# A gated attention and MLP decode step on one core: the first weight load in two transfers, TensorE's loop in eleven rounds, the output weight in other parts

## The chip, the core and the metric

The kernel runs on one core of one Trainium2 chip. The core has five engines with instruction streams of their own: TensorE (PE in the profile, with its weight loads as PEld), VectorE (DVE), ScalarE (ACT), GpSimd (POOL) and SyncE (SP). Data comes from device memory (HBM) by DMA: here every transfer is issued by SyncE, and the work of one transfer is spread over the core's 16 DMA engines. The on-chip memory that the engines read (SBUF) has 128 partitions, which are the rows of every tile.

The metric is the device time of one execution in microseconds. Before the change it is 676.03 us, the median of three runs (675.99 to 676.4).

## The reference

One decode step for two sequences (B = 2), one new token each, with a model width of D = 448. Branch A is attention over a cache of 4096 positions with 16 heads of 256, branch B is an MLP with a ReLU, and a gate mixes the two:

```python
def _A_ref(x, k_cache, v_cache, wq, wo):
    q = (x @ wq).reshape(B, Sq, H, Dh) -> (0, 2, 1, 3)
    scores = einsum("bhqd,bhkd->bhqk", q, k_cache) * Dh ** -0.5
    p = softmax(scores)
    o = einsum("bhqk,bhkd->bhqd", p, v_cache)
    return o @ wo
def _B_ref(x, w1, w2):
    return maximum(x @ w1, 0) @ w2
g = sigmoid((x * gate_w).sum(-1))
out = g * _A_ref(...) + (1 - g) * _B_ref(...)
```

Everything is float32. The caches are by far the largest inputs: 2 x 16 x 4096 x 256 elements each, 134 MB for the keys and as much for the values.

## The kernel before

**Units.** A unit is one head of one sequence; there are U = 32. The host lays the keys and values of a unit side by side as one block of 128 rows with 16,384 floats each (65,536 bytes a row, 8.4 MB a unit). Three buffers of that size, `slot[0]` to `slot[2]` (`slot_49`, `slot_50` and `slot_51` in the instruction listings below), fill most of SBUF.

**The start.** SyncE issues three transfers at once (lines 67 to 69): the query weight `wq` with the input `x` and the gate weight in its last columns, 128 rows of 14,348 floats, into `slot[0]`; then unit 0 into `slot[1]` and unit 1 into `slot[2]`. When `wq` has landed, VectorE copies `x` in a repeated layout to `xr` (L336), TensorE computes the gate (L196) and in two halves the queries (L207), and ScalarE stores them in `qt`. When TensorE is done with `wq`, SyncE loads unit 2 into `slot[0]` (L160).

**The loop.** For each unit, TensorE multiplies the keys by the query (`unit_pe`, L121), VectorE takes the maximum (L135), ScalarE the exponential (L128) and copies the next unit's query (L130), and VectorE multiplies the values by the weights and sums them, in eight instructions (L141). The last of these counts the semaphore `freed` up; on that SyncE issues the transfer of the unit three later into the buffer that came free (L166). The engines' loops run `LOOP = 10` rounds of three units, and the last two units stand written out behind the loop.

**The end.** The last unit's block is loaded as two halves (L171, L172). When unit 29's buffer `slot[0]` is free, the MLP's weights `wm` follow into it in two halves (L174, L175); when unit 30's buffer `slot[1]` is free, the output weight `wo` follows in parts (L179), each with a semaphore of its own in `wo_in`. `wo` has 32 chunks of 448 columns, 1,792 bytes a row. The lists `ACC` and `DIRECT` set the parts: chunks of `ACC` are multiplied into the accumulator `acc` (L276), four chunks at a time in four column groups of TensorE, on top of the MLP's second product (L264); `acc` is copied to `a_sb` (L368) and its four groups are folded into `z` (L284); chunks of `DIRECT` are multiplied straight into `z`, each in four pieces of 112 columns (L289). Then `z` is copied (L370) and 16 of its rows are stored (L182).

**What sets the order.** The program is written out by hand: each engine's stream runs in the order of the code, and semaphores tie the streams together. SyncE's transfers all go to one DMA queue in the order in which they are issued.

The last rows of the width need care: 448 is three times 128 and 64 more. The three full blocks go through a contraction over 128 partitions (`KF = 3`). For the fourth, half a block, the host puts two halves of a weight's columns on top of each other, and `rows_of` picks the upper or the lower 64 partitions.

Of the kernel before, what the change touches and what calls it, by code (L numbers as in the profile page):

```python
# [13 lines left out]
CW = 512  # L14
ACC = (14, 9)
DIRECT = (4, 2, 2, 1)
FOLD_AT = 0


def gated_mix_decode(nc, wq, kv, wm, wo, out):  # L20
# [41 lines left out]
    slot_in = [ev() for _ in range(SLOTS)]  # L62
    last_v, w1_in, w2_in = ev(), ev(), ev()
    wo_in = [ev() for _ in ACC + DIRECT]
    scored, maxed, raised, queried, freed = (ev() for _ in range(5))

    sp.dma_start(slot[0][:, :wq.shape[1]], wq).then_inc(slot_in[0], 16)  # L67
    sp.dma_start(slot[1], kv[0]).then_inc(slot_in[1], 16)
# [5 lines left out]
    fold = sb("fold", P, RB, B)  # L74
    xr = sb("xr", P, KC, P // B, B)
    ge = sb("ge", P, 1)
# [24 lines left out]

    def rows_of(c, i=0):
        return slice(0, P) if c < KF else slice(i * HP, (i + 1) * HP)

    def x_of(r, c, n=R):
        return xr[r, c].rearrange("p r b -> p (r b)")[:, :n]

    xg = slot[0][:, NW:wq.shape[1]].rearrange("p (c b) -> p c b", c=KC)

    ident_0, ident_ok, par_ok = ev(), ev(), ev()  # L110
    x_ok, gate_mm, gate_ok, ge_ok, gp_ok, omg_ok = (ev() for _ in range(6))
# [32 lines left out]

    LOOP = (U - 2) // SLOTS
    U1 = LOOP * SLOTS

# [7 lines left out]
    with nc.Block(no_gpsimd_drain=True) as block:  # L155

        @block.sync
        def _(_e):
            sp.wait_ge(q_mm, 2)
            sp.dma_start(slot[0], kv[2]).then_inc(slot_in[0], 16)  # L160
            with nc.Fori(0, LOOP - 1, engines=(ET.SP,)) as r:
# [12 lines left out]
            sp.dma_start(w1, wm[:, :W1]).then_inc(w1_in, 16)  # L174
            sp.dma_start(w2, wm[:, W1:]).then_inc(w2_in, 16)  # L175
            sp.wait_ge(freed, U - 1)
            k = 0
            for n, s in zip(ACC + DIRECT, wo_in):
                sp.dma_start(w_o[:, k * D:(k + n) * D], wo[:, k * D:(k + n) * D]).then_inc(s, 16)  # L179
                k += n  # L180
            sp.wait_ge(res_ok, 1)
            sp.dma_start(out, res[0:7 * 15 + 1:7, :]).then_inc(out_sem, 16)  # L182

        @block.gpsimd
        def _(_e):
            pool.memset(ident, 0.0).then_inc(ident_0, 1)
            pool.wait_ge(ident_0, 1)
# [3 lines left out]
        @block.tensor  # L191
        def _(_e):
            pe.wait_ge(x_ok, 1)
            for c in range(KC):
                r = rows_of(c)
                m = pe.matmul(pa[:, :1], x_of(r, c, P), xg[r, c, B:], start=(c == 0), stop=(c == KC - 1))  # L196
            m.then_inc(gate_mm, 1)
            W = 2 * KF * DH
            for i in range(2):
                w = slot[0][:, i * NW // 2:(i + 1) * NW // 2]  # L200
                if i:
                    pe.wait_ge(q_ok, i)
                for c in range(KC):
                    for g in range(G):
                        r = rows_of(c, g // 2)
                        at = g * W + c * CW if c < KF else G * W + g % 2 * CW
                        m = pe.matmul(pb[g * R:(g + 1) * R, :], x_of(r, c), w[r, at:at + CW], start=(c == 0),  # L207
                                      stop=(c == KC - 1))
                m.then_inc(q_mm, 1)
                pe.wait_ge(q_ok, i + 1)  # L210
# [6 lines left out]
                m.then_inc(q_tr, 1)  # L217
            with nc.Fori(0, LOOP, 1, engines=(ET.PE,)) as r:
                for k in range(SLOTS):
                    s = (k + 1) % SLOTS  # L220
                    unit_pe(k, r * SLOTS + (k + 1), r * 16 + (32 if s == 0 else 16), s)
            for k in range(U - U1):
                s = (k + 1) % SLOTS
                unit_pe(k, U1 + k + 1, LOOP * 16 + 16, s)

            half = W1 // 2

            def hidden(lo, hi):
                for c in range(lo, hi):
                    for g in range(G):  # L230
                        j, i = divmod(g, 2)
                        at = i * half + (j * KF + c if c < KF else 2 * KF) * FG
                        r = rows_of(c, j)
                        m = pe.matmul(pa[g * R:(g + 1) * R, :FG], x_of(r, c), w1[r, at:at + FG], start=(c == 0),  # L234
                                      stop=(c == KC - 1))
                return m

# [4 lines left out]
            pe.transpose(pc[:U, P:2 * P], ls, ident).then_inc(ml_tr, 1)  # L242
            hidden(2, 3)
# [3 lines left out]
            hidden(3, 4).then_inc(hid_mm, 1)  # L247
            pe.wait_ge(os_ok, 1)
# [31 lines left out]
            for i, a in enumerate(DIRECT):  # L280
                if i == FOLD_AT:
                    pe.wait_ge(a_ok, 1)
# [4 lines left out]
                for _ in range(a):  # L287
                    for g in range(G):
                        m = pe.matmul(z[g * R:(g + 1) * R, :DG], o_of(k),  # L289
                                      w_o[:, k * D + g * DG:k * D + (g + 1) * DG], start=(k == n and FOLD_AT > 0),  # L290
                                      stop=(k == NO - 1))
                    k += 1
            m.then_inc(z_mm, 1)

        @block.scalar
        def _(_e):
# [10 lines left out]
            act.activation(qc[:, 1, :], qt[:, 0, :], AF.Copy).then_inc(queried, 1)  # L307
            with nc.Fori(0, LOOP, engines=(ET.Activation,)) as r:
                u0 = act.snap(r * SLOTS)
# [19 lines left out]
        def _(_e):  # L329
# [5 lines left out]
            dve.wait_ge(slot_in[0], 16)  # L335
            dve.tensor_copy(xr, xg[:, :, None, :B].to_broadcast([P, KC, P // B, B])).then_inc(x_ok, 1)  # L336
            dve.wait_ge(gate_ok, 1)
# [4 lines left out]
            dve.tensor_scalar(omg, gp, -1.0, 1.0, op0=ALU.mult, op1=ALU.add).then_inc(omg_ok, 1)  # L342
            with nc.Fori(0, LOOP, engines=(ET.DVE,)) as r:
                u0 = dve.snap(r * SLOTS)
# [86 lines left out]
```

## Time and profile before

| what | before |
|---|---|
| median of three runs | 676.03 us (675.99 to 676.4) |
| the profiled execution's own time | 675.96 us |
| its span, first to last instruction | 674.4 us |
| TensorE busy | 218.0 us (32%) |
| VectorE busy | 340.4 us (50%) |
| ScalarE busy | 46.3 us (7%) |
| data moved | 289.61 MB, 429 GB/s over the span |
| DMA queue of SyncE, share of 16 engines | 99.3% |

The profiled execution's own time lies 1.56 us above its span; that is time ahead of the first instruction and behind the last that the profile doesn't show. Times in the profile count from the span's start. A row of a group reads: line, engine, operation, result <- operands, shapes and how many; behind the bar the busy time, the mean of one in ns, and the idle time ahead of them with what ended it. In a row of a timeline, the first number is the start and the second the length, in us.

### The profile page before, as it was taken

The numbers are of one execution on the slowest core, as the hardware profiler recorded it, in microseconds if no ns is written. First come the engines' busy times: TensorE is split into PE (matmuls) and PEld (weight loads), VectorE is DVE, ScalarE is ACT, GpSimd is POOL, SyncE is SP. The second block draws the span as 40 slices with busy tenths as digits, with TensorE's granted clock in tenths as the row PEclk, the third lists the DMA queues.
The fourth block names the chain that finished last, engine by engine and source line by source line (L and its number), as shares of the span: only waits on it lengthen the run. The fifth ranks groups of instructions, "written<-read, shape, count | busy, mean of one in ns | idle before, by whom it ended". The sixth has DMA issues, their size and how long they took to land.

```text
span 674.4 us, 3971 instructions
## 1 busy us (share of the span) xinstructions
PE 218.0 (32%) x1309; PEld 53.4 (8%) x1309; DVE 340.4 (50%) x563; ACT 46.3 (7%) x107; POOL 0.7 (0%) x6
## 2 busy tenths in 40 slices
PE   0733221333332123333322233333222333332445
PEld 0200000000000000000000000000000000000012
DVE  0024566545455665544656654455666445456760
ACT  0010000000000000000000000000000000000110
POOL 0000000000000000000000000000000000000000
PEclk9975667767655666766666676665567667655869
DMA  9999999999999999999999999999999999999997
GB/s 381 428 436 435 436 435 435 435 435 435 435 435 435 435 435 435 435 435 435 431 435 435 435 435 435 435 435 435 435 431 435 435 435 435 435 435 408 423 439 303
DMA packets 6084, 289.61 MB, mean 429 GB/s; under 512 B 704, under 2 KB 832, under 8 KB 1216
## 3 DMA queue, kind: packets, MB, share of 16 engines
q1 hardware_dynamic: 6080, 289.55, 99.3%
q8 instruction: 3, 0.05, 0.0%
q14 instruction: 1, 0.01, 0.0%
HBM read 289.54 MB, written 0.01 MB: 429 GB/s over the span
## 4 chain that ended last, share of the span: by engine, by line
DMA 70%; DVE 13%; PE 10%; issue 6%; ACT 1%; DVEq 1%; SPq 0%; ACTq 0%
DMA slot<-in_kv 65%; DVE slot L141 11%; PE sc L121 9%; DMA slot<-in_wo 4%; DVE nm L135 2%; ACT p L128 1%; DVEq L141 1%; PE acc L276 0%; PE z L289 0%; SPq L166 0%; DVE a_sb L368 0%; DVEq L135 0%; ACTq L128 0%; PE z L284 0%; SPq L67 0%
## 5 line engine op out<-in xcount | busy, mean ns | idle before, releaser
L121 PE MATMUL sc<-slot,qc 128*32 128x512 f32 x1024 | 187.2, 898 | 413.1 <-DMA slot<-in_kv 413.1
L141 DVE SCALAR_TENSOR_TENSOR slot<-slot,p 128x1024 f32<-128x1024 f32 x256 | 295.9, 1222 | 47.2 <-ACT p L128 45.8
L135 DVE TENSOR_REDUCE nm<-sc 128x1024 f32 (+1 forms) x32 | 39.2, 1225 | 243.4 <-PE sc L121 243.4
L121 PEld LDWEIGHTS sc<-slot,qc 128*32 128x32 f32 x1024 | 42.0, 156 | 557.6 <-issue 538.6
L128 ACT ACTIVATE p<-sc,nm 128x1024 f32<-128x1024 f32 x32 | 35.6, 1113 | 563.2 <-DVE nm L135 563.2
L141 DVE DVE_READ_ACCUMULATOR slot<-slot,p (+1 forms) x256 | 21.3, 83 | 0.0
L207 PE MATMUL pb<-slot,xr 128*32 128x512 f32 (+1 forms) x64 | 9.5, 732 | 0.0
L336 DVE COPY xr<-slot 128x512 f32<-128x512 f32 x1 | 0.4, 426 | 17.9 <-DMA slot<-in_wq 17.9
L234 PE MATMUL pa<-slot,xr 128*32 128x448 f32 (+1 forms) x32 | 5.2, 761 | 12.3 <-DMA slot<-in_wm 12.3
L196 PE MATMUL pa<-slot,xr 128*128 128x1 f32 (+1 forms) x8 | 2.0, 357 | 20.7 <-DVE xr L336 20.7
L368 DVE COPY a_sb<-acc 128x448 f32<-128x448 f32 x1 | 0.6, 625 | 14.0 <-PE acc L276 14.0
L276 PE MATMUL acc<-slot,oc 128*32 128x448 f32 x46 | 5.6, 542 | 4.2 <-DMA slot<-in_wo 4.2
L128 ACT ACTIVATION_READ_ACCUMULATOR p<-sc,nm (+1 forms) x32 | 6.2, 193 | 0.0
L130 ACT ACTIVATE qc<-qt 128x2 f32 (+1 forms) x31 | 5.9, 192 | 0.0
L264 PE MATMUL acc<-slot,hr 128*32 128x448 f32 x28 | 3.2, 541 | 1.0 <-ACT hr L323 1.0
L196 PEld LDWEIGHTS pa<-slot,xr 128*128 128x128 f32 (+1 forms) x8 | 1.9, 322 | 20.7 <-DVE xr L336 20.7
L207 PEld LDWEIGHTS pb<-slot,xr 128*32 128x32 f32 (+1 forms) x64 | 2.0, 129 | 5.9 <-issue 5.9
L276 PEld LDWEIGHTS acc<-slot,oc 128*32 128x32 f32 x46 | 1.7, 109 | 8.1 <-issue 5.8
L234 PEld LDWEIGHTS pa<-slot,xr 128*32 128x32 f32 (+1 forms) x32 | 0.9, 140 | 14.8 <-DMA slot<-in_wm 13.2
L289 PE MATMUL z<-slot,oc 128*32 128x112 f32 x72 | 1.9, 259 | 0.0
L301 ACT ACTIVATE q<-pb 128x512 f32<-128x512 f32 x2 | 1.2, 597 | 9.1 <-PE pb L207 9.1
L364 DVE COPY oc<-pc 128x256 f32<-128x256 f32 x4 | 1.4, 418 | 0.7 <-PE pc L251 0.7
(45 smaller groups left out, 16.9 us busy)
## 6 DMA issues: line engine op xcount, KB each, us to landing
slot<-in_kv SPq DMA_DIRECT2D x2, 4096.0 KB, 34.9
slot<-in_wq SPq DMA_DIRECT2D x1, 7174.0 KB, 19.4
slot<-in_wm SPq DMA_DIRECT2D x2, 3136.0 KB, 31.2
slot<-in_wo SPq DMA_DIRECT2D x1, 3136.0 KB, 24.6
slot<-in_wo SPq DMA_DIRECT2D x1, 2016.0 KB, 29.0
slot<-in_wo SPq DMA_DIRECT2D x1, 896.0 KB, 30.7
slot<-in_wo SPq DMA_DIRECT2D x2, 448.0 KB, 31.6
slot<-in_kv SPq DMA_DIRECT2D x31, 39.7
```

The costliest lines, as they stand in the source:

```text
L121: m = pe.matmul(sc[g * R:(g + 1) * R, c * CW:(c + 1) * CW], qc[:, s, t:t + 1].to_broadcast([P, R]), slot[s][:, lo:lo + CW], start=(t == 0) ...
L128: act.activation(p, sc, AF.Exp, bias=nm[:, bass.ds(u, 1)], accum_out=ls[:, bass.ds(u, 1)]).then_inc(raised, 1)
L130: act.activation(qc[:, s_next, :], qt[:, bass.ds(u + 1, 1), :].rearrange("p o t -> p (o t)"), AF.Copy).then_inc(queried, 1)
L135: dve.tensor_reduce(nm[:, bass.ds(u, 1)], sc, axis=AX.X, op=ALU.max, negate=True).then_inc(maxed, 1)
L141: m = dve.scalar_tensor_tensor(v, v, 1.0, p, op0=ALU.mult, op1=ALU.mult, accum_out=ov[:, bass.ds(u, 1), j].rearrange("p o -> p o"))
L196: m = pe.matmul(pa[:, :1], x_of(r, c, P), xg[r, c, B:], start=(c == 0), stop=(c == KC - 1))
L207: m = pe.matmul(pb[g * R:(g + 1) * R, :], x_of(r, c), w[r, at:at + CW], start=(c == 0), stop=(c == KC - 1))
L234: m = pe.matmul(pa[g * R:(g + 1) * R, :FG], x_of(r, c), w1[r, at:at + FG], start=(c == 0), stop=(c == KC - 1))
L264: pe.matmul(acc[g * R:(g + 1) * R, :D], hr[:, k, :], w2[:, k * D:(k + 1) * D], start=(k < G), stop=False)
L276: m = pe.matmul(acc[g * R:(g + 1) * R, :D], o_of(k), w_o[:, k * D:(k + 1) * D], start=False, stop=(k >= n - G))
L289: m = pe.matmul(z[g * R:(g + 1) * R, :DG], o_of(k), w_o[:, k * D + g * DG:k * D + (g + 1) * DG], start=(k == n and FOLD_AT > 0), stop=(k = ...
L364: m = dve.tensor_copy(oc[:, h], pc[:, h * B * J:(h + 1) * B * J].rearrange("p (o b j) -> p j o b", o=1, b=B) .to_broadcast([P, J, RB, B]))
```

## The change

There are four edits.

1. **wq in two transfers.** The first 16 rows (`FIRST`) are a transfer of their own with the semaphore `wq_in`; the other 112 rows follow as a second transfer on `slot_in[0]`. VectorE waits for both ahead of its first copy.
2. **The last half block as one contraction.** Instead of four products over 64 partitions, two over 128 partitions, each for 64 rows of the result: the left operand is the new tile `xl`, in which the other half is zero, and the host lays the weight's last columns out for it. A helper, `project`, serves the queries and the MLP's first product. `xr` keeps the three full blocks; VectorE makes `xl` and a small tile `xn` for the gate with three more copies, and GpSimd zeroes `xl`.
3. **TensorE in eleven rounds.** TensorE's loop covers all 32 units; in the last round a branch skips the third unit. The two units that stood written out behind it are gone. The other engines keep ten rounds and two units behind them (`LOOP` is now 11, and they run `LOOP - 1`).
4. **wo in other parts.** 14, 8 and 4 chunks go through `acc` and 3, 2 and 1 straight into `z`, where it was 14 and 9, and 4, 2, 2 and 1. There are six transfers as before.

```diff
-ACC = (14, 9)
-DIRECT = (4, 2, 2, 1)
-FOLD_AT = 0
+FIRST = 16
+ACC = (14, 8, 4)
+DIRECT = (3, 2, 1)
...
-    sp.dma_start(slot[0][:, :wq.shape[1]], wq).then_inc(slot_in[0], 16)
+    sp.dma_start(slot[0][:FIRST, :wq.shape[1]], wq[:FIRST]).then_inc(wq_in, 16)
+    sp.dma_start(slot[0][FIRST:, :wq.shape[1]], wq[FIRST:]).then_inc(slot_in[0], 16)
...
+    def project(dst, w, at, at_last, n, lo, hi):
+        for c in range(lo, min(hi, KF)):
+            for g in range(G):
+                m = pe.matmul(dst[g * R:(g + 1) * R, :n], x_of(c), w[:, at(c, g):at(c, g) + n], start=(c == 0), stop=False)
+        if hi == KC:
+            for i in range(2):
+                m = pe.matmul(dst[i * HP:(i + 1) * HP, :n], xl.rearrange("p j r b -> p (j r b)"),
+                              w[:, at_last(i):at_last(i) + n], start=False, stop=True)
+        return m
...
-    LOOP = (U - 2) // SLOTS
-    U1 = LOOP * SLOTS
+    LOOP = -(-U // SLOTS)
+    FULL = U - (LOOP - 1) * SLOTS
+
+    U1 = (LOOP - 1) * SLOTS
...
-            with nc.Fori(0, LOOP, 1, engines=(ET.PE,)) as r:
-                for k in range(SLOTS):
-                    s = (k + 1) % SLOTS
-                    unit_pe(k, r * SLOTS + (k + 1), r * 16 + (32 if s == 0 else 16), s)
-            for k in range(U - U1):
-                s = (k + 1) % SLOTS
-                unit_pe(k, U1 + k + 1, LOOP * 16 + 16, s)
+            with nc.Fori(0, LOOP, engines=(ET.PE,)) as r:
+                u0 = pe.snap(r * SLOTS)
+
+                def units(lo, hi):
+                    for k in range(lo, hi):
+                        unit_pe(k, u0 + (k + 1), r * 16 + (32 if k == SLOTS - 1 else 16), (k + 1) % SLOTS)
+
+                units(0, FULL)
+                with pe.If_lt(pe.to_reg(r), LOOP - 1):
+                    units(FULL, SLOTS)
+                pe.end_ifs()
...
-            dve.tensor_copy(xr, xg[:, :, None, :B].to_broadcast([P, KC, P // B, B])).then_inc(x_ok, 1)
+            dve.wait_ge(wq_in, 16)
+            dve.tensor_copy(xr, xg[:, :KF, None, :B].to_broadcast([P, KF, P // B, B]))
+            dve.tensor_copy(xn, xg[:, KF:, :B].to_broadcast([P, P // B, B]))
+            dve.wait_ge(xl_0, 1)
+            for j in range(2):
+                m = dve.tensor_copy(xl[j * HP:(j + 1) * HP, j], xg[j * HP:(j + 1) * HP, KF:, :B]
+                                    .to_broadcast([HP, RB, B]))
+            m.then_inc(x_ok, 1)
```

The order of the instructions moves at three places. The first is SyncE's start; `e` with a number is a semaphore, and the 128x14348 block is `wq`. Before:

```order
L67 DMA slot_49<-in_wq 128x14348 [waits barrier_Pool_Activation_PE_DVE_SP_release]
L68 DMA slot_50<-in_kv 128x16384
L69 DMA slot_51<-in_kv 128x16384
L157 UNCONDITIONAL_BRANCH
L160 DMA slot_49<-in_kv 128x16384 [waits e26]
```

And now, on the same engine:

```order
L67 DMA slot_49<-in_wq 16x14348 [waits barrier_Pool_Activation_PE_DVE_SP_release]
L68 DMA slot_49<-in_wq 112x14348
L69 DMA slot_50<-in_kv 128x16384
L70 DMA slot_51<-in_kv 128x16384
L169 UNCONDITIONAL_BRANCH
L172 DMA slot_49<-in_kv 128x16384 [waits e28]
```

One transfer more stands ahead of the two units, and the first of the two touches 16 partitions alone.

The second place is TensorE's loop; the products into `sc` are a unit's 16, and `e0`, `e1` and `e2` count the landings of the three buffers. Before, the loop's third unit, its end and the first of the two units behind it:

```order
L115 REGISTER_ALU
L116 REGISTER_ALU [waits e0]
L121 MATMUL sc<-slot_49,qc 32x512 [waits e15]
L121 MATMUL sc<-slot_49,qc 32x512 x15
L218 REGISTER_ALU
L218 COMPARE_AND_BRANCH
L121 MATMUL sc<-slot_50,qc 32x512 [waits e15,e1]
L121 MATMUL sc<-slot_50,qc 32x512 x15
```

Now, from the loop's second unit to its end and the first instruction behind it:

```order
L131 MATMUL sc<-slot_51,qc 32x512 x15
L233 COMPARE_AND_BRANCH
L125 REGISTER_ALU
L126 REGISTER_ALU [waits e0]
L131 MATMUL sc<-slot_49,qc 32x512 [waits e16]
L131 MATMUL sc<-slot_49,qc 32x512 x15
L233 UNCONDITIONAL_BRANCH
L225 REGISTER_ALU
L225 COMPARE_AND_BRANCH
L111 MATMUL pa<-slot_49,xr 32x448 [waits e5]
```

Two branches stand around the third unit, and the MLP's first product follows the loop directly.

The third place is TensorE's end, from the second part of `wo` on; before, `e7` to `e11` are the landings of `wo`'s second to sixth part, and `e45` is VectorE's copy to `a_sb`:

```order
L276 MATMUL acc<-slot_50,oc 32x448 [waits e7]
L276 MATMUL acc<-slot_50,oc 32x448 x8
L284 MATMUL z<-a_sb,fold 32x112 [waits e45]
L284 MATMUL z<-a_sb,fold 32x112 x3
L289 MATMUL z<-slot_50,oc 32x112 [waits e8]
L289 MATMUL z<-slot_50,oc 32x112 x15
L289 MATMUL z<-slot_50,oc 32x112 [waits e9]
L289 MATMUL z<-slot_50,oc 32x112 x7
L289 MATMUL z<-slot_50,oc 32x112 [waits e10]
L289 MATMUL z<-slot_50,oc 32x112 x7
L289 MATMUL z<-slot_50,oc 32x112 [waits e11]
L289 MATMUL z<-slot_50,oc 32x112 x3
```

Now, with `e8` to `e12` as those landings and `e47` as the copy:

```order
L281 MATMUL acc<-slot_50,oc 32x448 [waits e8]
L281 MATMUL acc<-slot_50,oc 32x448 x7
L281 MATMUL acc<-slot_50,oc 32x448 [waits e9]
L281 MATMUL acc<-slot_50,oc 32x448 x3
L289 MATMUL z<-a_sb,fold 32x112 [waits e47]
L289 MATMUL z<-a_sb,fold 32x112 x3
L294 MATMUL z<-slot_50,oc 32x112 [waits e10]
L294 MATMUL z<-slot_50,oc 32x112 x11
L294 MATMUL z<-slot_50,oc 32x112 [waits e11]
L294 MATMUL z<-slot_50,oc 32x112 x7
L294 MATMUL z<-slot_50,oc 32x112 [waits e12]
L294 MATMUL z<-slot_50,oc 32x112 x3
```

Three chunks have moved from the products into `z` (nine chunks of four pieces) to those into `acc`, ahead of the copy and the fold; the last part is still one chunk.

More of the change, by code (lines that the diff above doesn't have):

```diff
@@ L160, in _ @@
             sp.dma_start(slot[0], kv[2]).then_inc(slot_in[0], 16)
-            with nc.Fori(0, LOOP - 1, engines=(ET.SP,)) as r:
+            with nc.Fori(0, LOOP - 2, engines=(ET.SP,)) as r:
                 u0 = sp.snap(r * SLOTS)
@@ L199, in _ @@
             for i in range(2):
-                w = slot[0][:, i * NW // 2:(i + 1) * NW // 2]
                 if i:
                     pe.wait_ge(q_ok, i)
[L203 to L209, printed above, removed]
+                project(pb, slot[0][:, i * NW // 2:(i + 1) * NW // 2], lambda c, g: g * W + c * CW,
+                        lambda i: G * W + i * CW, CW, 0, KC).then_inc(q_mm, 1)
                 pe.wait_ge(q_ok, i + 1)
@@ L217, in _, with pe_tail @@
                 m.then_inc(q_tr, 1)
[L218 to L224 removed]
+            with nc.Fori(0, LOOP, engines=(ET.PE,)) as r:
[7 more added lines that the diff above has]
+                pe.end_ifs()
+        def pe_tail():
             half = W1 // 2
             def hidden(lo, hi):
[L229 to L236, printed above, removed]
+                return project(pa, w1, lambda c, g: g // 2 * half + (g % 2 * KF + c) * FG,
+                               lambda i: i * half + 2 * KF * FG, FG, lo, hi)
             pe.wait_ge(w1_in, 16)
@@ L289, in _ @@
                         m = pe.matmul(z[g * R:(g + 1) * R, :DG], o_of(k),
-                                      w_o[:, k * D + g * DG:k * D + (g + 1) * DG], start=(k == n and FOLD_AT > 0),
+                                      w_o[:, k * D + g * DG:k * D + (g + 1) * DG], start=False,
                                       stop=(k == NO - 1))
@@ L307, in _ @@
             act.activation(qc[:, 1, :], qt[:, 0, :], AF.Copy).then_inc(queried, 1)
-            with nc.Fori(0, LOOP, engines=(ET.Activation,)) as r:
+            with nc.Fori(0, LOOP - 1, engines=(ET.Activation,)) as r:
                 u0 = act.snap(r * SLOTS)
@@ L342, in _ @@
             dve.tensor_scalar(omg, gp, -1.0, 1.0, op0=ALU.mult, op1=ALU.add).then_inc(omg_ok, 1)
-            with nc.Fori(0, LOOP, engines=(ET.DVE,)) as r:
+            with nc.Fori(0, LOOP - 1, engines=(ET.DVE,)) as r:
                 u0 = dve.snap(r * SLOTS)
@@ L410 @@
     full, last = blocks(B_w1)
-    full = full.reshape(P, KF, 2, 2, FG).transpose(0, 3, 2, 1, 4).reshape(P, 2, -1)
-    last = last.reshape(HP, 2, 2, FG).transpose(1, 0, 2, 3).reshape(P, 2, FG)
+    full = full.reshape(P, KF, 2, 2, FG).transpose(0, 2, 3, 1, 4).reshape(P, 2, -1)
+    last = last.reshape(HP, 2, 2, FG).transpose(2, 0, 1, 3).reshape(P, 2, FG)
     w1 = np.concatenate([full, last], 2).reshape(P, -1)
```

35 lines of the change are left out of this document (20 added, 15 removed).

## The prediction

> **What bounds the kernel now.** I read the page's utilization part first, then the waits, then DMA by stretches, and last the chain of the end.
>
> ```profile
> span 674.4 us, 3971 instructions
> PE 218.0 (32%) x1309; PEld 53.4 (8%) x1309; DVE 340.4 (50%) x563; ACT 46.3 (7%) x107; POOL 0.7 (0%) x6
> ...
> q1 hardware_dynamic: 6080, 289.55, 99.3%
> q8 instruction: 3, 0.05, 0.0%
> ...
> DMA 70%; DVE 13%; PE 10%; issue 6%; ACT 1%; DVEq 1%; SPq 0%; ACTq 0%
> ...
> L121 PE MATMUL sc<-slot,qc 128*32 128x512 f32 x1024 | 187.2, 898 | 413.1 <-DMA slot<-in_kv 413.1
> ```
>
> No engine is busy for more than half of the span, while SyncE's queue holds the 16 DMA engines for 99.3% of it. TensorE stands idle for 413.1 us, all of it waiting for a unit to land. So the kernel lasts as long as its bytes do, plus what lies ahead of the first byte and behind the last.
>
> ```profile
> DMA packets 4320, 251.62 MB, mean 434 GB/s; under 512 B 479, under 2 KB 479, under 8 KB 479
> ...
> q1 hardware_dynamic: 4318, 251.59, 100.1%
> ...
> 660.00:662.00 2.00, 0.00 (x0) 0.00 (x0) 0.00 (x0) 0.00 (x0) 0.00 (x0) 1.00 1.02 436
> 669.00:670.00 1.00, 0.34 (x1) 0.00 (x0) 0.62 (x1) 0.00 (x0) 0.00 (x0) 1.00 0.85 333
> 670.00:671.00 1.00, 0.94 (x40) 0.94 (x44) 0.01 (x1) 0.00 (x0) 0.00 (x0) 1.00 0.23 90
> 671.00:672.00 1.00, 1.00 (x52) 0.94 (x40) 0.00 (x0) 0.00 (x0) 0.00 (x0) 1.00 0.05 18
> ```
>
> The first two lines are the stretch from 20 to 600 us: 251.59 MB in 580 us at a share of 1.001 make 251.59 / (1.001 x 16 x 580) = 27.1 GB/s for one of the 16 engines. The packets say how a transfer is shared out: 251.59 MB are some 3,839 rows of 65,536 B, and 479 packets are small; that is 128 rows and 16 small packets for each of 30 transfers, so every engine carries 8 rows and closes with a small packet. In the last four lines (the last two columns are DMA share and GB/s), the queue runs dry: at 670 to 671 us a share of 0.23 still moves 90 GB/s, or 90 / (0.23 x 16) = 24.5 GB/s for each busy engine, in packets of a few kB. An engine gets no faster when three quarters of them rest. So the limit isn't one that all 16 share. It is either the engine's own or that of the group of partitions it writes. In every large transfer here one engine goes with one share of the 128 partitions, so these rows can't tell the two apart. The forecast hangs on that.
>
> **The first transfer.** Before, `wq` is one transfer:
>
> ```profile
> 0.75 0.39 SPq L67 DMA_DIRECT2D slot<-in_wq  x1
> ...
> slot<-in_wq SPq DMA_DIRECT2D x1, 7174.0 KB, 19.4
> ...
> out<-res SPq DMA_DIRECT2D x1, 7.0 KB, 1.7
> ...
> q1 hardware_dynamic: 32, 0.01, 1.8%
> ```
>
> It lands at 0.75 + 19.4 = 20.15 us; its 7.35 MB take 16.9 us at 434 GB/s, so about 3.2 us pass without bytes. One row is 7174 KB / 128 = 57,392 B, 2.12 us of an engine. The last two rows are the kernel's own transfer of 16 rows, the result: 32 packets, so 16 rows with 16 small packets; sixteen rows, too, go to 16 engines, one each. The new first transfer thus keeps all 16 engines busy, each with one row, but all of them write to partitions 0 to 15.
>
> If the limit is the engine's own, this costs nothing: 2.12 us for the first rows, seven rows on each engine behind them, the same total. SyncE issues one transfer more (0.39 to 0.43 us), which puts unit 0's issue at some 1.65 us in place of 1.2; cover is the first row, which runs past 4 us. A gain at the start is bounded by the 3.2 us without bytes less the 1.14 us at which the first issue is over: 0 to 2.1 us. The nearest row, the store of 16 rows, needs 1.7 us from issue to landing for 7 KB, so a small transfer doesn't begin at once either; I take 0.
>
> If the limit belongs to groups of partitions, sixteen ways of 27.1 GB/s serve 128 partitions, eight each. Sixteen neighbours then lie on anything from 16 ways (dealt out one by one) down to two (eight neighbours on each): the first rows take between 2.12 and 8 x 2.12 = 16.95 us. Until they are done the other ways stand idle, and since each way must still carry its sixteenth of all bytes at a rate that it already holds for 99% of the span, that idle time comes back in full at the end: 0 with 16 ways, up to 16.95 us with two. Of the doublings 16, 8, 4 and 2, I take four ways, in the upper middle: four rows on each, 4 x 2.12 = 8.47 us. The second transfer gives each engine 7 rows, which fit neither groups of 4 nor of 8, so two engines meet on a way now and then. That costs from 0 to 7 x 2.12 = 14.8 us where they meet on all seven; I take one row, 2.1 us, near the low end, because engines that meet fall out of step and then meet less. Together +10.6 us.
>
> The Trainium skill, SBUF — State Buffer, section "Door 1: The DMA port swizzle (why `[64,N]` ≈ `[32,N]`)", says that DMA bandwidth goes by how many of 16 SBUF ports the partitions reach, that four consecutive partitions share one, and that partitions 0 to 15 reach four ports, measured at 104 GB/s. By it the first 0.92 MB would take 8.8 us (an estimate from that page's figure). No run here shows it, and the trace agrees only in that one engine's rate is what the page gives for one port.
>
> I side with the groups. For the engine's own limit speaks only that it is the simpler reading; for the groups speaks that every busy engine in the trace holds one rate to the end, and that all transfers before were spread over all partitions, so that this kernel never ran the other case.
>
> **The projections.** Each half of the queries takes 28 instructions in place of 32 (12 products of two passes and two more, for 16), the MLP's first product the same. VectorE makes four copies for one of 0.43 us, under 1 us more at worst. Cover is the wait for unit 0:
>
> ```profile
> 20.21 0.43 DVE L336 COPY xr<-slot 128x512 f32<-128x512 f32 x1 [17.94 <-DMA slot<-in_wq]
> ...
> 39.64 5.61 PE L121 MATMUL sc<-slot,qc 128*32 128x512 f32 x32 [4.87 <-DMA slot<-in_kv]
> ```
>
> TensorE waits 4.87 us for unit 0, so neither gain nor loss reaches the end: 0. A later `wq` leaves that cover, since unit 0 is behind it in the same queue and comes later by as much. In the MLP's product TensorE waits for `wo` afterwards: 0. GpSimd's zeroing of `xl` has 18 us.
>
> **The loop.** Two branches and a few register instructions in each of ten rounds, well under 1 us a round, fall into the 413.1 us of waiting (12.9 us a unit): 0. TensorE's program loses two units of 32 passes with their weight loads, 128 instructions, and some 60 more at the ends. The page has three fetches of instructions (the q8 row) of 16 KB; one may go. The stretch of the end has two of them:
>
> ```profile
> q8 instruction: 2, 0.03, 0.3%
> ```
>
> That is 630 to 674.4 us, so 0.003 x 16 x 44.4 = 2.1 us for two, about 1.1 us of one DMA engine each. At the end the slowest engines are some 1.4 us behind the rest (share 0.23 and 0.05 above). Removing one of three such delays helps only if it sat on the very last engine, from 0 to 1.4 us; with two fetches left I take 0.
>
> **The end.** The chain behind the last transfers:
>
> ```profile
> 637.84 29.02 DMA slot<-in_wo
> 666.86 0.04 issue
> 666.90 2.46 PE acc L276 x18
> 669.36 0.02 issue
> 669.38 0.64 DVE a_sb L368
> 670.02 0.04 issue
> 670.06 0.40 PE z L284 x8
> 670.46 1.77 PE z L289 x72
> 672.23 0.02 issue
> 672.25 0.28 DVE res L370
> ...
> L179 SPq DMA_DIRECT2D slot<-in_wo x6: 328/432/433, 637.5 to 639.7; - x6
> ...
> slot<-in_wo SPq DMA_DIRECT2D x1, 896.0 KB, 30.7
> slot<-in_wo SPq DMA_DIRECT2D x2, 448.0 KB, 31.6
> slot<-in_wo SPq DMA_DIRECT2D x1, 224.0 KB, 32.0
> ```
>
> Chunk 23 lands at 666.86, chunk 27 at about 638.3 + 30.7 = 669.0, so a chunk takes 0.54 us and chunk 26, the new end of `ACC`, lands at about 668.5. Four chunks are 8 passes at 2.46 / 18 = 0.14 us, done at 669.6 (0.24 us later than now); copy and fold follow (0.64 + 0.40 and two hops), to 670.7; then 48 passes for 72 at 1.77 / 72 = 0.025 us, to 671.9. The last chunk lands at 639.7 + 32.0 = 671.7 as before, since bytes, rows and number of parts are the same, and its 8 passes and the latency of the last one end by 672.1 to 672.2. So the chain of products, which now ends at 672.23, stops being what comes last by 0.05 us, and the landing takes over: -0.05.
>
> **Sum.** The profiled execution took 675.96 us; its median of runs stands 0.07 above it. 675.96 + 10.6 - 0.05 + 0 (projections, loop, fetch) = 686.5 us.
>
> **The rivals.**
>
> *No change.* If 27.1 GB/s is the engine's own limit, 675.96 - 0.05 = 675.9 us, with 0.4 us either way for the start. For it: the busy engines keep their rate, and the bytes and parts are equal.
>
> *Faster.* The rows flow as soon as the first short issue is over, or the fetch that goes was the one on the last engine: up to 2.1 or 1.4 us off, so down to 673.8 us. Against it: both need the whole bound; it is faster by over 0.2% only from 1.35 us on.
>
> *Slower in another way.* If the skipped third unit made TensorE's stream fetch anew in every round, ten fetches of 1.1 us on one DMA engine give +11 us, 687 us; spread over the engines they give about +1. The Trainium skill, Runtime: NRT & Kernel Launch, section "Instruction fetch mechanics", has a taken branch to outside the loaded window force a fetch of the target page. Against it here: ten rounds with a taken branch at each end came with three fetches in all (the q8 row).
>
> **How the numbers follow.** Groups of partitions 0.58; no change 0.34; faster 0.05; fetches 0.03. The likeliest gives 686.5 us; its own range goes from eight ways (4.24 us idle, no meeting) at 680 to two ways at 693. Over all cases, 675.0 to 691.0 leaves out the faster case, a little of no change, and the worst of the groups, some 0.15 in all. 0.2%, or 1.35 us, is about what a measurement of this kernel can tell from no change: faster 0.05, same 0.34, slower 0.61.
>
> **What would show it.** If the groups limit, DMA in the stretch from 4 to 10 us falls to about a quarter of 434 GB/s, `wq` lands at 28 us or later instead of 20.2, VectorE's first copy stands there, units land some 10 us later throughout at the same 434 GB/s, and the end looks as before, shifted. If `wq` lands at 20.2 us again, the groups are wrong and the time is 675.9. More than three q8 packets would show the fetches. For the end, the last products into `z` should follow the last landing by under 0.1 us, and the copy to `a_sb` should come some 0.2 us later against the last landing than now. What would make the forecast wrong is above all that a way into SBUF carries more than one engine brings, or that the first rows don't share one.

## The result and the profile after

The changed kernel takes 694.01 us, the median of four runs (693.39 to 695.05), against 676.1 us before (675.99 to 676.4, also four runs). The ratio is 1.0265, with a 95% interval of 1.0253 to 1.0277: 17.9 us slower. The forecast was 686.5 us: it had the direction and the kind of mechanism, but its range ended at 691.

The profiled execution's span is 692.1 us, 17.7 us longer than before. Its page shows where the time isn't:

```profile
span 692.1 us, 3931 instructions
PE 217.9 (31%) x1279; PEld 52.7 (8%) x1279; DVE 340.9 (49%) x566; ACT 46.4 (7%) x107; POOL 0.8 (0%) x7
...
GB/s 159 265 417 421 432 428 451 443 428 424 424 436 451 443 428 424 424 436 451 443 424 428 424 436 451 443 424 428 424 432 447 451 424 428 424 432 432 431 431 296
...
q1 hardware_dynamic: 6096, 289.55, 99.2%
q8 instruction: 3, 0.05, 0.0%
...
L131 PE MATMUL sc<-slot,qc 128*32 128x512 f32 x1024 | 186.9, 897 | 411.6 <-DMA slot<-in_kv 411.6
```

TensorE has 30 instructions less, the engines are busy as before, the bytes are the same, and TensorE's wait for units even fell by 1.5 us. What differs are the first two of the forty slices: 159 and 265 GB/s, where every later one but the last holds 417 or more. Note the share of the queue: 99.2%, as if nothing were wrong. A packet that takes longer still counts as a busy engine, so the share doesn't show that the engines are slow.

The stretches of the start say it more closely (the last two columns are DMA share and GB/s; bytes count where their packet begins):

```profile
0.00:10.00 10.00, 0.00 (x0) 0.00 (x0) 0.74 (x3) 1.28 (x1) 0.79 (x7) 1.00 1.09 161
10.00:38.00 28.00, 0.00 (x0) 0.00 (x0) 0.00 (x0) 0.00 (x0) 0.00 (x0) 1.00 0.93 242
...
60.00:600.00 540.00, 163.96 (x896) 36.69 (x892) 293.43 (x476) 36.33 (x84) 0.00 (x0) 0.62 1.00 435
```

From 10 to 38 us the queue holds the engines for 0.93 of their time and moves 242 GB/s; from 60 us on it is the old rate. Before the change, the first 20 us were:

```profile
0.00:10.00 10.00, 0.00 (x0) 0.00 (x0) 0.74 (x3) 1.28 (x1) 0.70 (x6) 1.00 0.91 367
10.00:20.00 10.00, 0.00 (x0) 0.00 (x0) 0.00 (x0) 0.00 (x0) 0.00 (x0) 1.00 1.09 472
```

The issues of `wq` and VectorE's first copy (from the timeline and the list of DMA issues; in the latter the last number is us from issue to landing):

```profile
0.75 0.41 SPq L67 DMA_DIRECT2D slot<-in_wq  x1
1.22 0.41 SPq L68 DMA_DIRECT2D slot<-in_wq  x1
...
slot<-in_wq SPq DMA_DIRECT2D x1, 6277.2 KB, 37.7
slot<-in_wq SPq DMA_DIRECT2D x1, 896.8 KB, 11.0
...
38.92 0.55 DVE L347 COPY xr<-slot 128x384 f32<-128x384 f32 x1 [36.64 <-DMA slot<-in_wq]
```

The sixteen rows land at 0.75 + 11.0 = 11.8 us and the other 112 at 1.22 + 37.7 = 38.9 us. Before, all 128 had landed at 20.15 us. So 18.7 us are lost by the time `wq` is there, and 17.7 of them are still there at the end.

### The profile page after: what moved, and what is told of

The parts are those of the page before. It is cut to its first block, busy times and chain, and to the rows that moved or that the text cites. A ratio compares the mean times of both kernels' runs of the same rounds, so it can differ in the third digit from the quotient of the medians.

```text
span 692.1 us, 3931 instructions
## 1 busy us (share of the span) xinstructions
PE 217.9 (31%) x1279; PEld 52.7 (8%) x1279; DVE 340.9 (49%) x566; ACT 46.4 (7%) x107; POOL 0.8 (0%) x7
## 3 DMA queue, kind: packets, MB, share of 16 engines
q1 hardware_dynamic: 6096, 289.55, 99.2%
## 4 chain that ended last, share of the span: by engine, by line
DMA 66%; DVE 13%; PE 12%; issue 6%; ACT 1%; DVEq 1%; another core or an unknown queue 1%; SPq 0%; ACTq 0%
DMA slot<-in_kv 56%; DVE slot L151 10%; PE sc L131 10%; DMA slot<-in_wq 5%; DMA slot<-in_wo 4%; DVE nm L145 2%; PE pb L111 1%; ACT p L138 1%; DVEq L151 0%; PE pb L114 0%; PE pa L208 0%; PE z L294 0%; PE pc L223 0%; ACT q L311 0%
## 5 line engine op out<-in xcount | busy, mean ns | idle before, releaser
L208 PE MATMUL pa<-slot,xr 128*128 128x1 f32 x6 | 1.4, 356 | 39.9 <-DVE xl L351 39.9
L111 PE MATMUL pb<-slot,xr 128*32 128x512 f32 x48 | 8.0, 817 | 0.0
L111 PE MATMUL pa<-slot,xr 128*32 128x448 f32 x24 | 4.2, 820 | 11.8 <-DMA slot<-in_wm 11.8
L208 PEld LDWEIGHTS pa<-slot,xr 128*128 128x128 f32 x6 | 1.4, 326 | 39.9 <-DVE xl L351 39.9
L114 PE MATMUL pb<-slot,xl 128*64 128x512 f32 x8 | 2.2, 618 | 0.0
L111 PEld LDWEIGHTS pb<-slot,xr 128*32 128x32 f32 x48 | 1.7, 137 | 4.0 <-issue 4.0
## 6 DMA issues: line engine op xcount, KB each, us to landing
slot<-in_wq SPq DMA_DIRECT2D x1, 6277.2 KB, 37.7
```

What stands on the lines that cost most here:

```text
L111: m = pe.matmul(dst[g * R:(g + 1) * R, :n], x_of(c), w[:, at(c, g):at(c, g) + n], start=(c == 0), stop=False)
L114: m = pe.matmul(dst[i * HP:(i + 1) * HP, :n], xl.rearrange("p j r b -> p (j r b)"), w[:, at_last(i):at_last(i) + n], start=False, stop=True)
L208: m = pe.matmul(pa[:, :1], x_of(c, P) if c < KF else xn[r].rearrange("p r b -> p (r b)"), xg[r, c, B:], start=(c == 0), stop=(c == KC - 1))
```

## The experiments

### The split alone, and everything but the split

The first pair asks which of the four edits it is. One kernel is the one before with only the split:

```diff
-    sp.dma_start(slot[0][:, :wq.shape[1]], wq).then_inc(slot_in[0], 16)
+    sp.dma_start(slot[0][:FIRST, :wq.shape[1]], wq[:FIRST]).then_inc(wq_in, 16)
+    sp.dma_start(slot[0][FIRST:, :wq.shape[1]], wq[FIRST:]).then_inc(slot_in[0], 16)
...
             dve.wait_ge(slot_in[0], 16)
+            dve.wait_ge(wq_in, 16)
```

> The kernel before with the split of wq alone. If the split is the whole loss: 693.5 to 694.5 us, wq lands at about 38.9 us. If part of the loss is in the loop, the projections or the parts of wo, clearly less than 694.

Measured: 693.77 us (693.44 to 694.52), ratio 1.0266 (1.025 to 1.0282). The other is the changed kernel with the single transfer back:

```diff
-    sp.dma_start(slot[0][:FIRST, :wq.shape[1]], wq[:FIRST]).then_inc(wq_in, 16)
-    sp.dma_start(slot[0][FIRST:, :wq.shape[1]], wq[FIRST:]).then_inc(slot_in[0], 16)
+    sp.dma_start(slot[0][:, :wq.shape[1]], wq).then_inc(slot_in[0], 16)
...
-            dve.wait_ge(wq_in, 16)
```

> The changed kernel with wq as one transfer of 128 rows again. If the split is the whole loss: 675.5 to 676.3 us, no different from before. If the other three edits cost anything that the profile hid: above 677.

Measured: 676.21 us (675.83 to 676.8), ratio 1.0001 (0.9992 to 1.001). The split is the whole loss, and the other three edits together are worth nothing that can be measured. Its page has one fetch of instructions less (the q8 row):

```profile
span 674.4 us, 3929 instructions
...
q8 instruction: 2, 0.03, 0.0%
```

Two fetches in place of three, and the same span of 674.4 us as before the change. The shorter program of TensorE needn't be the reason: the changed kernel has the same one, and three fetches.

### The same bytes, split by columns

Is it that there are two transfers, or where the first one writes? Here the first transfer has the bytes of sixteen rows, taken as 1,792 columns of all 128:

```diff
-FIRST = 16
+FIRST = 1792
...
-    sp.dma_start(slot[0][:FIRST, :wq.shape[1]], wq[:FIRST]).then_inc(wq_in, 16)
-    sp.dma_start(slot[0][FIRST:, :wq.shape[1]], wq[FIRST:]).then_inc(slot_in[0], 16)
+    sp.dma_start(slot[0][:, :FIRST], wq[:, :FIRST]).then_inc(wq_in, 16)
+    sp.dma_start(slot[0][:, FIRST:wq.shape[1]], wq[:, FIRST:]).then_inc(slot_in[0], 16)
```

> The changed kernel with wq split by columns: the first 1,792 columns of all 128 rows (0.92 MB, the bytes of sixteen rows), then the other 12,556. Ways theory: every engine writes its own share of the partitions in both transfers, so 675.5 to 676.5 us and wq lands at 20.2 to 20.6. Rival, a second transfer for wq is itself what costs: near 694 us.

Measured: 676.46 us (675.81 to 676.65), ratio 1.0004 (0.9995 to 1.0013). Its issues of `wq`:

```profile
slot<-in_wq SPq DMA_DIRECT2D x1, 6278.0 KB, 18.9
...
slot<-in_wq SPq DMA_DIRECT2D x1, 896.0 KB, 4.5
```

The same 0.92 MB land in 4.5 us, 6.5 us sooner than as sixteen rows, and the rest 18.9 us after its issue. A second transfer is free. It brings nothing either: the first bytes of the queue come no sooner in a way that the end would show.

### Rows of transfers measured alone

A kernel without the computation issues thirteen transfers of 57,392 B a row, one after the other. The edit is its program, which for each set of rows is:

```python
sp.dma_start(buf[n % 2][ROWS[n], :N], kv[n][ROWS[n], :N]).then_inc(sems[n], 16)
sp.wait_ge(sems[n], 16)
```

> This kernel leaves all of the computation out: it issues thirteen transfers of rows of 57,392 B one after another, each waited for before the next, and stores zeros. The sets of partitions are 0-127; 0-15; sixteen in steps of 8, of 7 and of 4; 16-127; 0-111; 0-63; the 64 even ones; 0-31; 32 in steps of 4; 0-95; 0-127 again. Ways theory (sixteen ways into the partitions, neighbours share one): all 128 land in about 19.4 us as wq did before; sixteen neighbours in 9 to 11 us, sixteen in steps of 8 or 4 in 6 to 7 us, in steps of 7 in 4.6 to 6.7 us; 0-63 about as long as all 128 (19 us) though it is half the bytes; 32 in steps of 4 clearly sooner than 0-31. Rival, only the number of rows counts (any transfer that isn't 128 rows is slow, wherever its rows lie): the four transfers of sixteen rows agree within 0.5 us, and so do the two of 64 and the two of 32.

In SyncE's timeline each row is an issue, and the next one follows when it has landed, so the differences of the starts are the times (some are left out; the table has all):

```profile
0.73 0.39 SPq L40 DMA_DIRECT2D buf<-in_kv  x1
20.23 0.35 SPq L42 DMA_DIRECT2D buf<-in_kv  x1
30.64 0.59 SPq L44 DMA_DIRECT2D buf<-in_kv  x1
...
51.34 0.33 SPq L50 DMA_DIRECT2D buf<-in_kv  x1
80.69 0.32 SPq L52 DMA_DIRECT2D buf<-in_kv  x1
109.47 0.50 SPq L54 DMA_DIRECT2D buf<-in_kv  x1
129.63 0.51 SPq L56 DMA_DIRECT2D buf<-in_kv  x1
140.93 0.32 SPq L58 DMA_DIRECT2D buf<-in_kv  x1
...
```

| partitions | rows | us to landing |
|---|---|---|
| 0-127 | 128 | 19.5 and 20.0 |
| 0-15 | 16 | 10.4 |
| in steps of 8, of 7, of 4 | 16 | 7.2, 6.8, 6.7 |
| 16-127 | 112 | 29.4 |
| 0-111 | 112 | 28.8 |
| 0-63 | 64 | 20.2 |
| the even ones | 64 | 11.3 |
| 0-31 | 32 | 11.0 |
| 0-124 in steps of 4 | 32 | 7.2 |
| 0-95 | 96 | 28.1 |

Not the number of rows counts but where they lie: 64 neighbours take as long as all 128, and the 64 even rows about half of that. And 112 rows take 9 to 10 us longer than 128. The sixteen rows in steps of 7 and of 8 took 0.1 to 0.2 us more than expected (6.8 for at most 6.7, 7.2 for at most 7); the control of 128 rows came out as `wq` had.

### Which partitions share a way

A second kernel of the kind takes pairs and small sets.

> This kernel, too, leaves out all of the computation. Seventeen transfers of rows of 57,392 B, each waited for before the next: partition 0 alone; 0 and 1; 0 and 2; 0 and 4; 0 and 8; 0 and 16; 0 and 32; 0 and 64; 0-3; 0, 4, 8, 12; 0, 32, 64, 96; 0-28 in steps of 4; 64-92 in steps of 4; 0-112 in steps of 16; 0-47; 0-94 in steps of 2; all 128. A row takes an engine 2.12 us, and about 2.5 us pass around it, so what doesn't share lands in 4.5 to 5 us and what shares a way in two in 6.6 to 7.2 us. Ways theory, with a way for four neighbours and those 32 further: 0 and 1, 0 and 2, and 0 and 32 share, the other pairs don't; 0-3 takes about 10 to 11 us (four rows on one way); 0, 4, 8, 12 doesn't share; 0, 32, 64, 96 shares in two; 0-28 in steps of 4 doesn't share, and neither does 64-92 although other engines write there. Rival, an engine is slow wherever it writes outside its own share of the partitions: 64-92 is as slow as a shared set (6.6 us or more) and 0 with 64 too.

```profile
0.73 0.32 SPq L39 DMA_DIRECT2D buf<-in_kv  x1
4.97 0.24 SPq L41 DMA_DIRECT2D buf<-in_kv  x1
11.12 0.72 SPq L43 DMA_DIRECT2D buf<-in_kv  x1
18.01 0.56 SPq L45 DMA_DIRECT2D buf<-in_kv  x1
22.99 0.56 SPq L47 DMA_DIRECT2D buf<-in_kv  x1
27.73 0.56 SPq L49 DMA_DIRECT2D buf<-in_kv  x1
32.67 0.49 SPq L51 DMA_DIRECT2D buf<-in_kv  x1
39.27 0.48 SPq L53 DMA_DIRECT2D buf<-in_kv  x1
43.95 0.26 SPq L55 DMA_DIRECT2D buf<-in_kv  x1
53.93 0.64 SPq L57 DMA_DIRECT2D buf<-in_kv  x1
...
```

In the order of the list, up to 0-3 as shown and from there on from the rows left out: 0 alone 4.2 us; 0 and 1 6.2; 0 and 2 6.9; 0 and 4 5.0; 0 and 8 4.7; 0 and 16 4.9; 0 and 32 6.6; 0 and 64 4.7; 0-3 10.0; 0, 4, 8, 12 5.0; 0, 32, 64, 96 6.2; 0-28 in steps of 4 4.7; 64-92 in steps of 4 4.9; 0-112 in steps of 16 7.1. So 0 shares with 1, 2, 3 and 32 and not with 4, 8, 16 and 64: every set shares or doesn't as the ways theory said, though 0 alone, 0 and 1, and 0, 32, 64, 96 came in 0.3 to 0.4 us under the times expected.

Against the rival, that an engine is slow wherever it writes outside its own share, speak 0 and 64 and above all 64-92, which is as fast as 0-28; it falls if both sets go to the same engines, which no run shows. Another rival is where the rows are read, since in these kernels the places in device memory change along with the partitions. But the rows of `kv` lie 65,536 B apart and those of `wq` 57,392 B, and the sets behave alike in both: rows 0-15 took 10.4 us here and 10.7 from `wq` (in the run with the first transfer by itself, below), rows 16-127 took 29.4 and 30.7. That speaks for the partitions.

The Trainium skill, SBUF — State Buffer, section "Door 1: The DMA port swizzle (why `[64,N]` ≈ `[32,N]`)", has just this map, of sixteen ports for four neighbours and the four 32 further on; these runs agree with it.

### The same in the kernel: even and odd rows, and halves

Two splits into 64 and 64 rows, which differ only in where the rows lie:

```diff
+    sp.dma_start(slot[0][0:P - 1:2, :wq.shape[1]], wq[0:P - 1:2]).then_inc(wq_in, 16)
+    sp.dma_start(slot[0][1:P:2, :wq.shape[1]], wq[1:P:2]).then_inc(slot_in[0], 16)
```

> The changed kernel with wq split into its 64 even rows and then its 64 odd rows. The 64 even rows ran at full rate alone (11.28 us to landing, against 20.15 us for rows 0-63). Ways theory: no loss, 675.8 to 676.8 us, wq lands at 20.2 to 20.6. Rival, a split of the rows is what costs, wherever they lie: over 685 us.

Measured: 676.74 us (676.36 to 677.62), ratio 1.0008 (0.9998 to 1.0017). And the neighbours:

```diff
-FIRST = 16
+FIRST = 64
```

> The changed kernel with wq split into rows 0-63 and then rows 64-127. Ways theory: two engines on each of eight ways in both transfers, 8 rows of 4.24 us for 2.12, that is 16.9 us of loss: 692 to 694 us, wq lands near 37. Rival, a split of the rows costs by its number of transfers: the same as the even and odd rows.

Measured: 695.18 us (694.74 to 695.9), ratio 1.0281 (1.0264 to 1.0298). That is 18.8 us, somewhat over the 16 to 18 expected. A transfer of rows 0-63 alone shows the reason: its 64 rows took 20.2 us at a share of 0.88, which is 0.88 x 16 x 20.2 / 64 = 4.4 us a row, rather than 4.24.

```profile
51.34:80.69 29.35, 0.00 (x0) 0.00 (x0) 1.00 0.89 219
109.47:129.63 20.16, 0.00 (x0) 0.00 (x0) 1.00 0.88 182
129.63:140.93 11.30, 0.00 (x0) 0.00 (x0) 1.00 0.82 325
```

These are the stretches of rows 16-127, of 0-63 and of the 64 even ones in the first kernel of transfers alone. By the same sum a row costs 3.7 us with 16-127, and 2.3 us with the even ones.

### Each of the two transfers by itself

To price the two transfers apart, the kernel before gets one transfer more ahead of everything, into the third buffer; unit 1 waits for it before it is loaded there. `wq` stays one transfer.

```diff
+    sp.dma_start(slot[2][:16, :wq.shape[1]], wq[:16]).then_inc(probe_in, 16)
     sp.dma_start(slot[0][:, :wq.shape[1]], wq).then_inc(slot_in[0], 16)
     sp.dma_start(slot[1], kv[0]).then_inc(slot_in[1], 16)
+    sp.wait_ge(probe_in, 16)
     sp.dma_start(slot[2], kv[1]).then_inc(slot_in[2], 16)
```

> The kernel before, with sixteen rows of wq loaded once more ahead of everything else, into partitions 0-15 of the third buffer, whose unit waits for them; wq itself is one transfer of 128 rows. This isolates the first transfer. Its 0.92 MB alone are 2.1 us. Ways theory: the four ways that it uses take 7.4 to 8.5 us, and the other twelve can't make that good later: 683.4 to 684.9 us. Rival, the idle ways catch up in the 650 us that follow: 678 us.

Measured: 683.98 us (683.85 to 684.21), ratio 1.0117 (1.0098 to 1.0135): 7.9 us more than the 676.1 before, of which 2.1 are bytes. Nothing is caught up in the 650 us that follow. The other 112 rows in its place:

```diff
-    sp.dma_start(slot[2][:16, :wq.shape[1]], wq[:16]).then_inc(probe_in, 16)
+    sp.dma_start(slot[2][16:, :wq.shape[1]], wq[16:]).then_inc(probe_in, 16)
```

> The kernel before, with rows 16-127 of wq loaded once more ahead of everything else, into partitions 16-127 of the third buffer; wq itself is one transfer of 128 rows. This isolates the second transfer. Its 6.43 MB take 14.8 us at the full rate. If the second transfer is what the prediction priced too low, it costs the 27 us that 112 rows took alone: 702 to 704.5 us; net of its bytes 12 to 13 us, and with the 5.6 us net of the first transfer the two make the 17.9 us of the changed kernel. If the two cost that only together (the engines leave the first transfer out of step), 691 to 695 us.

Measured: 702.4 us (702.22 to 703.71), ratio 1.0393 (1.0374 to 1.0412): 26.4 us more, 11.6 over the bytes. And as a control, all 128 rows:

```diff
+    sp.dma_start(slot[2][:, :wq.shape[1]], wq).then_inc(probe_in, 16)
```

> The control: all 128 rows of wq loaded once more ahead of everything else, into the third buffer. 7.35 MB at the full rate are 16.9 us, and every engine writes its own share of the partitions: 692.7 to 693.7 us. So sixteen rows more than in the run with rows 16-127 should take about 10 us less.

Measured: 693.43 us (693.01 to 693.64), ratio 1.0253 (1.0235 to 1.0272): 17.4 us more, about the price of its bytes at full rate (16.9). Sixteen rows more are 9 us cheaper. Net of their bytes the parts add up: 5.8 + 11.6 = 17.4 us, against the 17.9 of the change; so each costs by itself, not through the other.

### Does a shared way slow its neighbours?

With seven rows for each of 16 engines, few of them should meet. Why are all 112 rows slow?

> All computation is left out here as well. Twelve transfers of rows of 57,392 B, each waited for before the next: 0-28 in steps of 4 (eight rows, none shares a way); 0-35 in steps of 5 (eight rows, 0 and 35 share, six don't); 0-30 in steps of 5 (seven rows, none shares; they may all go to fewer engines); 0, 33 and 66 (the first two share); 0 and 33; sixteen in steps of 7 (two pairs share, twelve rows don't); 0-21 in steps of 3 (two pairs of eight share); 16-127; 0-79; 0-63; the 64 even ones; all 128. Read is the mean time of a packet, share x 16 x length of the stretch / number of rows; alone, a first row takes about 2.65 us. Theory A, only the engines that share a way slow down: 0-35 in steps of 5 averages (6 x 2.65 + 2 x 4.4) / 8 = 3.1 us, and 0, 33 and 66 (2 x 4.4 + 2.65) / 3 = 3.8 us. Theory B, a shared way slows engines beside it too: 0-35 in steps of 5 averages 3.7 us or more, and 16 rows in steps of 7 stay at 4.0 us. Under B the second transfer of 112 rows is explained: seven rows on each engine, two ways in each step shared, and all engines at some 3.9 us a row.

The sets of eight rows in steps of 4, of eight and of seven in steps of 5, of three, of sixteen in steps of 7 and of eight in steps of 3, by stretches (a set of two is left out):

```profile
0.73:5.58 4.85, 0.15 (x1) 0.00 (x0) 1.00 0.26 95
5.58:11.99 6.41, 0.00 (x0) 0.00 (x0) 1.00 0.24 72
11.99:16.99 5.00, 0.00 (x0) 0.00 (x0) 1.00 0.24 80
16.99:23.48 6.49, 0.00 (x0) 0.00 (x0) 1.00 0.11 27
...
29.98:36.40 6.42, 0.00 (x0) 0.00 (x0) 1.00 0.55 143
36.40:43.30 6.90, 0.00 (x0) 0.00 (x0) 1.00 0.28 67
```

The mean packet is 2.5 us for the eight that don't share, 0.24 x 16 x 6.41 / 8 = 3.1 us for the eight with one pair, 2.7 us for the seven, and 0.11 x 16 x 6.49 / 3 = 3.8 us for the three: this is theory A, where a shared way slows only those on it. The sixteen in steps of 7, which hold two pairs, average 0.55 x 16 x 6.42 / 16 = 3.5 us here (and 0.59 x 6.82 = 4.0 us in the first kernel of this kind), over the 3.1 of A. The eight in steps of 3, with two pairs as well, average 0.28 x 16 x 6.90 / 8 = 3.9 us, where A gives (4 x 4.4 + 4 x 2.65) / 8 = 3.5; in the trace's records of single packets none of these eight is under 3.3 us. So A holds with one pair and fails with two; B fails with one pair, for which it has 3.7 us or more in the eight in steps of 5.

The 112 rows show the same step by step. The sixteen engines begin each of their rows within 2.7 us of one another, so that a stretch of 3 us can be laid around the sixteen starts of a step (306 GB/s are sixteen rows), and share x length is the mean time of a row in it. Rows 16-127, alone, in the first kernel of this kind:

```profile
52.00:55.00 3.00, 0.00 (x0) 0.00 (x0) 1.00 1.27 306
55.00:58.00 3.00, 0.00 (x0) 0.00 (x0) 1.00 1.37 306
59.00:62.00 3.00, 0.00 (x0) 0.00 (x0) 1.00 1.06 306
62.50:65.50 3.00, 0.00 (x0) 0.00 (x0) 1.00 1.05 306
66.00:69.00 3.00, 0.00 (x0) 0.00 (x0) 1.00 1.30 306
69.50:72.50 3.00, 0.00 (x0) 0.00 (x0) 1.00 1.36 306
73.00:76.00 3.00, 0.00 (x0) 0.00 (x0) 1.00 1.30 306
```

That is 3.8, 4.1, 3.2, 3.2, 3.9, 4.1 and 3.9 us, 26.1 us together, where seven rows at 2.12 make 14.8. It fits one way of dealing: each engine takes seven neighbouring rows, in order. Then two ways are shared in five of the steps (in the first by rows 16 and 51 and by 72 and 107), and only one in the third (88 and 123) and in the fourth (68 and 103), which are the fast ones. For rows 0-111 the same count puts the steps with one shared way fourth and fifth, and there the seven means are 3.7, 4.2, 4.1, 3.0, 3.3, 3.9 and 3.9 us.

The trace's single packets say who is slow. In the steps with one pair, two of the sixteen take 3.8 to 4.2 us and the other fourteen 2.5 to 3.5. In the steps with two pairs all sixteen take over 3.1 us, and most of them about 4, though only four share a way. If only the rows that meet paid, 4.4 us for 2.12, the loss would be 24 x 2.28 / 16 = 3.4 us, and it is over 11.

Smaller blocks of neighbours agree. 80 rows took 24.1 us, and 48 rows 23.3 us, longer than all 128 in the same kernel (19.6), where the 48 even rows took 15.1; dealt in order, up to three of the 48 neighbours meet on a way, and after the first row every engine takes 6.8 to 7.3 us a row. The dealing in order is inferred from these steps. It can't hold for all 128 rows, the 64 even ones or the 32 in steps of 4, which would then meet in pairs at each step, and which ran at 2.2 to 2.5 us a row. What holds up the engines that share no way stays open.

## Why the prediction was right, and where it failed

**The choice between engine and partitions** was right. The prediction found that the trace of before can't tell the engine's own limit from that of a group of partitions, since every transfer in it gave each engine its own share, and it took the groups. The pairs and the column split show that it is the groups. The two reasons that it took from the trace fit the engine's own limit as well, so on the trace alone the choice was a guess. The rival without change falls with 693.77 us for the split alone and 676.46 us for the same bytes in columns, and with it the faster case.

**The first transfer** was priced a little high. The prediction had four ways at four rows each, 8.47 us. Four ways is right (0-3 share, 0, 4, 8 and 12 don't), and a lucky pick as far as the trace of before goes. But in the 8.47 us each engine also moves one of the eight rows that it had to move before, so by the prediction's own figures the loss is 8.47 - 2.12 = 6.35 us, as the second transfer is priced at the other seven. In the column split the same bytes land 6.5 us sooner, and the transfer by itself adds 7.9 us with its 2.1 us of bytes, 5.8 net. That idle ways can't make their time good later was right: 17.7 of the 18.7 us that `wq` is late are still there at the end.

**The second transfer** is the step that failed. Of bounds from 0 to 14.8 us the prediction took one row, 2.1 us, with the reason that "engines that meet fall out of step and then meet less". The transfer alone adds 11.6 us over its bytes, and in the changed kernel it lasts from 11.8 to 38.9 us, 27.1 us, against 14.9 us in the column split (from 5.2 to 20.1). That is 12.2 us where 2.1 stood. The reason fails twice. The engines did not fall out of step enough to miss each other: they still begin their seventh row within 2.5 us of one another (31.1 to 33.6 us). And it isn't only engines that meet that pay: by the same stretches of 3 us the seven steps take 4.8, 4.1, 2.8, 3.3, 3.8, 4.0 and 3.9 us here, and in five of the seven steps all sixteen engines are slow, as in the transfer alone. The term's own upper bound held; the total's didn't, because the range ended at 691, below 675.96 + 8.47 + 14.8 = 699, the sum of the middle of the one term and the top of the other (697 with 6.35 for the first). With the terms as measured against the column split the sum is 675.96 + 6.5 + 12.2 = 694.7 us, and 694.01 was measured.

**Projections, loop and fetch** at 0 were right: without the split the other three edits measure 676.21 us, ratio 1.0001. The rival of extra fetches falls: three in the changed kernel, as before, and two in the one without the split. The cover of the projections held even with `wq` 18.7 us late: unit 0, behind it in the queue, still came last, and TensorE waited 3.7 us for it.

**The end** at -0.05 us is too small to be measured as a time: without the split, the products into `z` end at 672.32 us, against 672.23 before, in the same span. Of the changed kernel's chain:

```profile
655.63 30.30 DMA slot<-in_wo
...
685.97 1.00 PE acc L281 x8
...
687.00 0.64 DVE a_sb L385
...
687.68 0.40 PE z L289 x8
688.08 1.58 PE z L294 x48
```

The products into `z` end at 689.66, half a microsecond behind the last landing at about 689.2 (657.1 + 32.1), as they did before (672.23 after 671.7). That the landing takes over, as the prediction had it, shows in the single records: the products of the last chunk begin 0.04 us behind its landing, after a pause, where before they began 0.1 us behind it without one. The copy to `a_sb` starts 2.2 us ahead of the last landing, where it was 2.3; some 0.2 us later had been forecast.

**The signs** named ahead were right where they spoke of the start: `wq` at 38.9 us ("28 us or later"), the first copy with it, the units later by a fixed amount at the old rate. The stretch from 4 to 10 us was a poor sign, since bytes count where their packet begins and a packet of 7 us hides in it; the 242 GB/s from 10 to 38 us are the better one.

## What to carry to other kernels

A DMA that touches fewer than all 128 partitions can be slower than one of all 128, even with fewer bytes: look at where the rows lie before cutting a transfer by rows, and cut it by columns, which was free here. When the trace can't tell two limits apart because every transfer in it is of one kind, price every new transfer of the change by the slow reading, the large one first, and let the range reach the sum of the bounds. Don't price only the engines that meet: here two shared ways slowed all sixteen. And where a queue is the bound, its busy share doesn't show a slow start; bytes per time do.

## What the runs showed of the hardware

- Partition 0 shares its way into SBUF with 1, 2, 3 and 32 (6.2 to 6.9 us for two rows, 10.0 for 0-3), and not with 4, 8, 16 or 64 (4.7 to 5.0 us).
- 64 rows in neighbouring partitions take 20.2 us, 128 rows 19.5, the 64 even rows 11.3. Even rows and steps of 4 over all partitions run at 2.3 and 2.5 us a row, close to the 2.2 of all 128.
- 48, 96 and 112 neighbouring rows take 23.3, 28.1 and 29.4 us, longer than 128. In a step of 112 rows with one shared way (by the dealing inferred above), two of sixteen engines take about 4 us a row and the rest about 3; with two shared ways nearly all take about 4. Why isn't shown.
- One fetch of 16 KB of instructions more or less (three against two) made no difference to the span of 674.4 us.
